# Strassen's seven products for the output GEMM of the second MLP too

## The chip, the core and the metric

The kernel runs on one core of a Trainium2 chip. Five engines work side by side: TensorE (PE) multiplies into PSUM banks, and its weight loads (PEld) overlap with it; VectorE (DVE), ScalarE (ACT) and GpSimd (POOL) compute on tiles; SyncE (SP) issues most DMAs. The metric is the device time of the whole program in microseconds; lower is better.

## The reference

Three stages run one after the other. Attention has 8 batches and 8 heads over 576 positions of 64 channels, with keys and values averaged in groups of 8. Its result is reshaped to 4608 rows of 512 and goes through two MLPs, all in float32:

```python
h = x @ w_in                                   # first MLP, 512 -> 2048 -> 512
g = np.where(h >= 1, h, np.where(h <= -1, 0.0, (h + 1) ** 2 / 4))
x = (g @ w_out).astype(np.float32)
gate = 1.0 / (1.0 + np.exp(-(x @ w_gate)))     # second MLP, 512 -> 1536 -> 512
val = x @ w_val
return (gate * val @ w_out).astype(np.float32)
```

## The kernel before

**Arithmetic.** Float32 values are split into a high and a low fp32r part: ScalarE writes the high part by a cast, VectorE the low part by a subtraction. `three` multiplies such pairs in three matmuls of 128x128 weights by 512 columns (high by high, high by low, low by high), so that any term costs three of them.

**Stages.** The 4608 rows are nine blocks of 512 (`TB`), kept transposed. Attention and the first MLP end at about 930 us of the trace. In the second MLP, block 0 is done plainly (`prepare`, `out_part`). Meanwhile `prepare` forms, for each of six groups `i` of two hidden tiles (`MP` = 6) and for gate and value (`n`), the seven weight combinations of Strassen's scheme in Winograd's form, and spills them to `seven` in HBM, 1792 KB for each `i` and `n`. Blocks 1 to 8 are then done in four pairs (`pr`).

**A pair.** Both input GEMMs use the seven products: for each `i` and `n` there are seven calls of the inner `product`, of six matmuls each. That is 6 x 2 x 7 x 6 = 504 matmuls a pair. Each product starts in one of four banks, `h` or `a`; VectorE adds (`add`) join the products outside PSUM, ScalarE copies one of them out (L917), and `finish` adds, takes the sigmoid (ScalarE, L903) or multiplies by it (VectorE, L910) into a `gs` tile. The output GEMM is plain: for each block and each of 12 hidden tiles, `out_part` splits `gs` (ScalarE L781, VectorE L782) and `three` adds into four `acc` banks, 2 x 12 x 4 x 3 = 288 matmuls a pair. Then `out_rows` copies the four banks to SBUF and stores rows of 512 floats.

**What sets the order.** Each call of `op` or `op2` records an operation with an engine, a cost, a due time (`key`), and the tiles that it reads and writes. `Plan.issue` then simulates the engines and writes every engine's instructions in the order in which its own times let them start, earliest due time first among those that could start together. On the chip each engine runs its list strictly in that order and waits on semaphores. The weights of one (`i`, `n`) come back in a single DMA (`load_seven`) to the three slots `wa`, `wa`, `wb`; SP's list holds these loads, the loads of `y` blocks and the stores.

Of the kernel before, what the change touches and what calls it, by code (L numbers as in the profile page):

```python
# [8 lines left out]
F32 = mybir.dt.float32  # L9
# [9 lines left out]
P = 128  # L19
# [45 lines left out]
class Plan:  # L65
# [7 lines left out]
    def op(self, eng, cost, key, fn, r=(), w=(), after=(), behind=(), nbytes=0, share=1.0, dmas=1):  # L73
# [24 lines left out]
        o.data, o.order = data, order - data  # L98
# [98 lines left out]
def pooled_attention_two_mlps(  # L197
# [46 lines left out]
    one, att, two = ExitStack(), ExitStack(), ExitStack()  # L244
# [424 lines left out]

    pools2 = {}  # L670

    def second_a():
        att.close()
        pools2["wa"] = two.enter_context(tc.tile_pool(name="wa", bufs=2))

    def second_b():
        one.close()
        pools2["right"] = two.enter_context(tc.tile_pool(name="two", bufs=1, side="right"))

    open_a = op("none", 0.0, 0.0, second_a, behind=att_ops)  # L680
    open_b = op("none", 0.0, 0.0, second_b, behind=one_ops)

    def late(tag, bufs, shape, dtype=F32, fifo=True):

        b = Buf(lambda: pools2["wa" if tag == "wa" else "right"], tag, bufs, shape, dtype, fifo)
        b.behind = [open_a if tag == "wa" else open_b]
        return b
# [5 lines left out]
    def buf_win(behind):  # L693
        b = Buf(win_p, "win", M1, [P, 2, TB], F32R)
        b.behind = behind
        return b
# [12 lines left out]
    PSTEP = 11 * 2.6  # L709
# [55 lines left out]
    def load_seven(n, i, key):  # L765
        sl, d = buf_seven(), seven[2 * i + n]
        op2(SP, 0.475, key, lambda: nc.sync.dma_start(
            out=sl.t.rearrange("p s k f -> p (s k f)").bitcast(F32), in_=d.t), r=[d], w=[sl], nbytes=P * 2 * NMAT * HK * 4)
        return sl
# [9 lines left out]
    def out_part(gs, m, key, accs, last, ahead=5):  # L779
        g = buf_g()  # L780
        op2(ACT, 0.62, key - ahead, lambda: nc.scalar.copy(out=g.t[:, 0], in_=gs.t), r=[gs], w=[g])  # L781
        op2(DVE, 0.69, key - ahead + 1, lambda: nc.vector.tensor_tensor(  # L782
            out=g.t[:, 1], in0=gs.t, in1=g.t[:, 0].bitcast(F32), op=ALU.subtract), r=[gs, g], w=[g])
# [6 lines left out]

    def buf_gs():
        return late("gs", 12, [P, TB], fifo=False)
# [9 lines left out]
    accs = [bank("acc") for _ in range(4)]  # L802
    for i in range(MP):
        slots = [prepare(n, i, due2(0, 2 * i) - 6 + 2.6 * n) for n in range(2)]
        T = due2(0, 2 * i)
        banks = {(n, f): bank("ha"[n], True) for n in range(2) for f in range(2)}
        for n in range(2):
            sl, a21 = slots[n]
            for f in range(2):
                last = []  # L810
                for c in range(KD):
# [5 lines left out]
                    last = [op(PE, 0.65, T + 5.2 * n + 2.6 * f + 0.1 * c, mm, r=[sl, a21, xs[c]], w=[banks[n, f]], behind=last)]  # L817
        for f in range(2):
            m = 2 * i + f
            t, gs = Buf(t_p, "t", 2, [P, TB]), buf_gs()  # L820
# [149 lines left out]
```

## Time and profile before

| what | value |
|---|---|
| median of 3 runs | 1752.68 us |
| the profiled execution | 1755.67 us |
| its span, first to last instruction | 1753.8 us |
| mean granted clock of TensorE | 0.995 |
| DMA, mean over the span | 134 GB/s |

The profiled execution took 3.0 us more than the median. A busy PE in the page is not PE at its peak, since the records of successive matmuls overlap; the spacing of their starts tells the pace. Times in the trace count from the first instruction.

### The profile page before, as it was taken

To read this page: it belongs to the slowest core of one execution; us is meant where nothing else is said; L and a number is where in the kernel's file an instruction comes from. 1 tells how busy PE (TensorE), PEld (TensorE's weight loads), DVE (VectorE), ACT (ScalarE), POOL (GpSimd) and SP (SyncE) were. 2 spreads that over 40 slices of the span, in tenths; PEclk is the share of its full clock that TensorE was granted. 3 is DMA by queue.
4 is the path that set the end of the run, shared out by engine and by line. 5 is a ranking of instruction groups with operands and counts; after the bars stand their busy time and mean duration, and the time that the engine had idled before them with its cause. 6 is when DMAs were issued, how large, how long until landed. Compare 5 with 4: busy or idle time off the path is not lost.

```text
span 1753.8 us, 24039 instructions
## 1 busy us (share of the span) xinstructions
PE 1723.8 (98%) x9016; PEld 1393.4 (79%) x9016; DVE 1051.5 (60%) x1874; ACT 805.7 (46%) x1786; POOL 52.7 (3%) x90
## 2 busy tenths in 40 slices
PE   7899999999999999999999999999999999999998
PEld 5676777778777778777887888888888888888887
DVE  5899867677776867574646645345444644464432
ACT  5876656566665656564755332123222312141212
POOL 0000001010010101010000000000000000000000
PEclk9999999999999999999999999999999999999999
DMA  7742525243443414031415875354344433443411
GB/s 205 229 119 69 149 57 163 62 134 97 116 116 92 134 45 134 16 128 40 174 39 202 318 291 204 126 192 145 126 146 166 149 119 146 166 167 126 150 43 49
DMA packets 148532, 234.37 MB, mean 134 GB/s; under 512 B 84160, under 2 KB 104640, under 8 KB 140736
## 3 DMA queue, kind: packets, MB, share of 16 engines
q1 hardware_dynamic: 138624, 182.50, 33.1%
q0 software_dynamic: 9792, 50.34, 7.9%
q8 instruction: 71, 1.16, 0.3%
q14 instruction: 45, 0.37, 0.1%
HBM read 173.02 MB, written 50.33 MB: 127 GB/s over the span
## 4 chain that ended last, share of the span: by engine, by line
PE 92%; DMA 3%; DVE 2%; ACT 1%; SPq 0%; issue 0%; DVEq 0%; ACTq 0%
PE acc L580 13%; PE h L580 13%; PE acc L582 13%; PE acc L581 13%; PE h L582 13%; PE h L581 12%; PE a L582 4%; PE a L581 4%; PE a L580 4%; PE a L484 2%; DMA raw<-in_moe_w_out_dram 1%; PE a L413 1%; DMA kv<-in_v_dram 1%; DMA x<-in_v_dram 1%; DMA xb<-y 0%
## 5 line engine op out<-in xcount | busy, mean ns | idle before, releaser
L580 PE MATMUL h<-x,win 128*128 128x512 f32 x576 | 231.2, 401 | 1.0 <-ACT win L505 1.0
L580 PE MATMUL acc<-g,wj 128*128 128x512 f32 x576 | 228.7, 397 | 1.2 <-ACT g L505 1.2
L582 PE MATMUL acc<-g,wj 128*128 128x512 f32 x576 | 225.4, 391 | 3.5 <-DVE wj L514 3.5
L582 PE MATMUL h<-x,win 128*128 128x512 f32 x576 | 225.7, 392 | 1.3 <-DVE win L514 1.3
L581 PE MATMUL acc<-g,wj 128*128 128x512 f32 x576 | 225.6, 392 | 1.0 <-DVE g L514 1.0
L581 PE MATMUL h<-x,win 128*128 128x512 f32 x576 | 225.5, 391 | 0.0
L781 ACT CAST g<-gs 128x512 fp32r<-128x512 f32 x108 | 66.8, 622 | 319.2 <-PE acc L582 200.4
L645 ACT ACTIVATE t<-h,half 128x512 f32<-128x512 f32 x144 | 99.2, 689 | 186.9 <-PE h L582 186.9
L582 PE MATMUL acc<-win,g 128*128 128x512 f32 x432 | 168.2, 389 | 2.1 <-DVE g L782 2.1
L580 PE MATMUL acc<-win,g 128*128 128x512 f32 x432 | 168.2, 389 | 0.0
L581 PE MATMUL acc<-win,g 128*128 128x512 f32 x432 | 168.1, 389 | 0.0
L782 DVE TENSOR_TENSOR g<-gs,g 128x512 fp32r<-128x512 f32 x108 | 74.1, 690 | 135.2 <-ACT g L781 135.0
L649 DVE SCALAR_TENSOR_TENSOR t<-t,h 128x512 f32<-128x512 f32 x144 | 97.3, 676 | 90.9 <-ACT t L647 90.8
L580 PEld LDWEIGHTS h<-x,win 128*128 128x128 f32 x576 | 108.7, 189 | 35.7 <-issue 9.7
L582 PEld LDWEIGHTS acc<-g,wj 128*128 128x128 f32 x576 | 108.4, 188 | 28.4 <-DVE wj L514 5.4
L580 PEld LDWEIGHTS acc<-g,wj 128*128 128x128 f32 x576 | 108.2, 188 | 27.8 <-ACT g L505 1.7
L582 PEld LDWEIGHTS h<-x,win 128*128 128x128 f32 x576 | 108.7, 189 | 25.9 <-DVE win L514 2.5
L581 PEld LDWEIGHTS acc<-g,wj 128*128 128x128 f32 x576 | 108.3, 188 | 23.2 <-DVE g L514 1.6
L581 PEld LDWEIGHTS h<-x,win 128*128 128x128 f32 x576 | 108.8, 189 | 21.1
L514 DVE TENSOR_TENSOR wj<-wout_f,wj 128x512 fp32r<-128x512 f32 x144 | 99.0, 688 | 33.3 <-ACT wj L505 33.0
L514 DVE TENSOR_TENSOR g<-t,g 128x512 fp32r<-128x512 f32 x144 | 98.8, 686 | 33.6 <-ACT g L505 33.1
L505 ACT CAST g<-t 128x512 fp32r<-128x512 f32 x144 | 89.1, 619 | 52.5 <-DVE t L649 50.1
(212 smaller groups left out, 3231.1 us busy)
## 6 DMA issues: line engine op xcount, KB each, us to landing
wa<-seven SPq DMA_DIRECT2D x32, 1792.0 KB
wb<-seven SPq DMA_DIRECT2D x16, 1792.0 KB
seven<-wa POOLq DMA_DIRECT2D x8, 1792.0 KB, 7.4
y<-raw SPq DMA_DIRECT2D x18, 512.0 KB
w<-f POOLq DMA_DIRECT2D x36, 256.0 KB, 2.5
out_dram<-raw SPq DMA_DIRECT2D x18, 512.0 KB
win<-in_moe_w_in_dram SPq DMA_DIRECT2D x16, 512.0 KB
raw<-in_moe_w_out_dram SPq DMA_DIRECT2D x16, 512.0 KB
```

Source lines behind the costliest of these rows:

```text
L413: nc.tensor.matmul(out=scs[h].t[r0 % P:r0 % P + D, r0 // P * C:r0 // P * C + C], lhsT=qT.t[D * h:D * h + D, r0:r0 + D], rhs=kts[b % 2, p]. ...
L484: nc.tensor.matmul(out=px.t[D * h:D * h + D, lo:hi], lhsT=vps[b % 2, p].t[:, h], rhs=rhs, start=True, stop=True)
L505: ACT: (0.52, lambda: nc.scalar.copy(out=dst.t[:, 0], in_=src())),
L514: op(engs, [0.6 if e == DVE else 1.23 for e in engs], key, [lambda e=e: by[e].tensor_tensor(out=dst.t[:, 1], in0=src(), in1=dst.t[:, 0].bi ...
L580: nc.tensor.matmul(out=o, lhsT=wh, rhs=xh, start=start, stop=False, skip_group_check=more)
L581: nc.tensor.matmul(out=o, lhsT=wh, rhs=xl, start=False, stop=False, skip_group_check=more)
L582: nc.tensor.matmul(out=o, lhsT=wl, rhs=xh, start=False, stop=stop, skip_group_check=more)
L645: op(ACT, 0.69, Tg, lambda t=t, hps=hps: nc.scalar.activation(out=t.t, in_=hps.t, func=AF.Relu, bias=half.t, scale=0.5), r=[hps, half], w=[t])
L649: op(DVE, 0.69, Tg + 2, lambda t=t, hps=hps: nc.vector.scalar_tensor_tensor(out=t.t, in0=t.t, scalar=1.0, in1=hps.t, op0=ALU.min, op1=ALU. ...
L781: op2(ACT, 0.62, key - ahead, lambda: nc.scalar.copy(out=g.t[:, 0], in_=gs.t), r=[gs], w=[g])
L782: op2(DVE, 0.69, key - ahead + 1, lambda: nc.vector.tensor_tensor(out=g.t[:, 1], in0=gs.t, in1=g.t[:, 0].bitcast(F32), op=ALU.subtract), r ...
```

## The change

The output GEMM of the four pairs goes by seven products too. A block of two hidden tiles and 512 outputs is a two by two of 128x256 blocks of the weight; the two blocks of the pair and the two hidden tiles make the other two by two. `out_pair` forms, in place in the tiles `hs` that hold the gated values, four combinations for each `i` (`sums`; VectorE or GpSimd, whichever the planner finds earlier), splits each operand afresh (L716, L717), and runs seven products of 6 x 6 matmuls, 252 a pair. Weights are now the stationary side, so results stand transposed and are turned on the way out: by VectorE's 32x32 block transposes with stores of 64 floats a row (`store`), or, for the last block half of all, by eight transposes on TensorE (`store_rows`).

`prepare_out` forms the seven combinations of the output weights during the first pair, from six reloads, and spills 42 tiles of 256 KB (`seven_o`). In the last pair the sixth and seventh products change places.

Where one product is to be added to another that is still needed alone, ScalarE copies the first from its bank into the next bank (`to_bank`) and TensorE adds the next product to it there. The gate and value products are rearranged in the same way. The weights of these come one product at a time (256 KB, 10 slots `ws`, rows of 1 KB), after the big slots `wa` and `wb` are closed (`second_c`). The combinations of the inputs (`minus`) may go to GpSimd. The planner's step for one `i` of a pair's input products is 27.3 us instead of 28.6 us (`PSTEP`).

```diff
-    PSTEP = 11 * 2.6
+    PSTEP = 10.5 * 2.6
+    def second_c():
+        zero.close()
+        zero_a.close()
+        pools2["ws"] = two.enter_context(tc.tile_pool(name="ws", bufs=10))
+        pools2["g2"] = two.enter_context(tc.tile_pool(name="g2", bufs=3))
+        pools2["wo"] = two.enter_context(tc.tile_pool(name="wo", bufs=5, side="right"))
...
+    def load_seven(n, i, mat, key):
+        w, d = late("ws", 10, [P, 2, HK], F32R), seven[2 * i + n]
+        op2(SP, 0.475, key, lambda: nc.sync.dma_start(
+            out=w.t.bitcast(F32), in_=d.t.rearrange("p (s k f) -> p s k f", s=2, k=NMAT)[:, :, mat]), r=[d], w=[w], nbytes=P * 2 * HK * 4)
...
+    def prepare_out(i, key):
+        a = Buf(raw_p, "raw", 2, [P, 4, HK], fifo=False)
+        sm = late("o", 2, [P, 4, HK])
...
+        comb(0, lambda: a.t[:, 1], lambda: a.t[:, 3], ALU.add)
+        comb(1, lambda: sm.t[:, 0], lambda: a.t[:, 0], ALU.subtract)
+        comb(2, lambda: a.t[:, 0], lambda: a.t[:, 1], ALU.subtract)
+        comb(3, lambda: a.t[:, 2], lambda: sm.t[:, 1], ALU.subtract)
+        for k in range(NMAT):
...
+            op2(PL, 1.0, key + 2 + k, lambda w=w, k=k: nc.gpsimd.dma_start(
+                out=seven_o[i][k].t, in_=w.t.rearrange("p s f -> p (s f)").bitcast(F32)), r=[w], w=[seven_o[i][k]], nbytes=P * 2 * HK * 4)
...
+    def out_pair(pr, hs, K0):
+        KP = PSTEP * MP / NMAT
...
+        def comb(key, h, n, x, y, alu, other=None):
+            op2((DVE, PL), (0.69, 1.3), key, [lambda e=e: by[e].tensor_tensor(out=h.t[:, n], in0=x(), in1=y(), op=alu) for e in (DVE, PL)],
+                r=[h] + ([other] if other else []), w=[h])
...
+        def product(n, mat, o, start, what):
+            chain = []
+            for i in range(MP):
+                key = K0 + KP * (n + i / MP)
...
+                split_to(key - 30, lambda src=src, b=b: src.t[:, b], lambda g=g: g.t[:, 0], lambda g=g: g.t[:, 1], 0.66, src, g)
...
+        def store(key, j, half, ct):
+            tr = Buf(raw_p, "raw", 2, [P, TB // 32, 2, 32])
+            for e in range(2):
+                op2(DVE, 0.63, key, lambda e=e: nc.vector.transpose(
+                    out=tr.t[:, :, e], in_=ct.t[:, e].rearrange("p (t i) -> p t i", i=32)), r=[ct], w=[tr])
+            for bl in range(4):
+                c0 = 2 * P * half + 64 * bl
+                op2(SP, 0.65, key + 20, lambda bl=bl, c0=c0: nc.sync.dma_start(
+                    out=out[j * TB:(j + 1) * TB, c0:c0 + 64].rearrange("(t j) i -> j t i", j=32),
...
+        product(0, 0, X, True, lambda k, h1, h2: (h1, 0))
+        s1 = o_buf()
+        to_sbuf(key(1) - 30, X, s1)
...
+        X2 = [bank("acc", True) for _ in range(2)]
+        to_bank(key(3) - 29, s1, X2)
...
+        product(4, 4, X2, False, lambda k, h1, h2: (h1, 0))
+        ct = c_buf()
+        add(key(5) - 30, ct, X2, s35)
...
+            Y2 = fourth()
+            ct = c_buf()
+            add(key(n4 + 1) - 30, ct, Y2, u3)
+            store_rows(key(n4 + 1) - 20, j1, 1, ct)
...
                 product(0, A, 0, B11, True)
-                op(ACT, 0.6, T + H * 1, lambda s1=s1, A=A: nc.scalar.copy(out=s1.t, in_=A.t), r=[A], w=[s1])
-                product(1, Bk, 4, T2, True)
-                add(T + H * 2, u2, Bk, s1)
-                product(2, Ck, 5, T3, True)
-                add(T + H * 3, u3, Ck, u2)
-                product(3, Dk, 3, T1, True)
-                finish(T + H * 4, (1, 1), Dk, u3)
-                product(4, A, 1, B21, False)
-                finish(T + H * 5, (0, 0), A, None)
-                product(5, Ck, 2, T4, False)
-                finish(T + H * 6, (1, 0), Ck, u2)
-                product(6, Dk, 6, B22, False)
-                finish(T + H * 7, (0, 1), Dk, u2)
...
+                to_bank(T + H * 1, A, Bk)
+                product(1, Dk, 3, T1, True)
+                op2(ACT, 0.6, T + H * 2 + 0.6, lambda u5=u5, Dk=Dk: nc.scalar.copy(out=u5.t, in_=Dk.t), r=[Dk], w=[u5])
+                product(2, Bk, 4, T2, False)
+                to_bank(T + H * 3, Bk, Ck)
+                op2(ACT, 0.6, T + H * 3 + 1, lambda u2=u2, Bk=Bk: nc.scalar.copy(out=u2.t, in_=Bk.t), r=[Bk], w=[u2])
+                product(3, A, 1, B21, False)
+                finish(T + H * 4, (0, 0), A, None)
+                product(4, Ck, 5, T3, False)
+                finish(T + H * 5, (1, 1), Ck, u5)
+                product(5, Dk, 6, B22, False)
+                finish(T + H * 6, (0, 1), Dk, u2)
+                product(6, Ck, 2, T4, False)
+                finish(T + H * 7, (1, 0), Ck, None)
```

What ScalarE's list holds in the third pair, while the products of that pair run, before (L903 sigmoids, L917 the copy of the first product to SBUF, L781 a high part for the output GEMM):

```order
L781 CAST g<-gs 128x512
L903 ACTIVATE t<-t 128x512
L903 ACTIVATE t<-h 128x512
L903 ACTIVATE f<-f 128x512
L781 CAST g<-gs 128x512
L903 ACTIVATE f<-f 128x512
L917 COPY f<-h 128x512
L781 CAST g<-gs 128x512 x2
L917 COPY f<-h 128x512
```

And in the changed kernel at the same place (L1113 `to_bank`, L1121 and L1124 copies to SBUF, L1102 sigmoids, L716 a high part for the output GEMM; `h` and `a` are PSUM banks):

```order
L1113 COPY h<-a 128x512
L1124 COPY u<-a 128x512
L1102 ACTIVATE t<-h 128x512
L1102 ACTIVATE t<-t 128x512
L1102 ACTIVATE f<-f 128x512
L1102 ACTIVATE f<-h 128x512
L1113 COPY a<-h 128x512
L716 CAST g_13215<-win 128x512
L1121 COPY u<-a 128x512
L1113 COPY h<-a 128x512
L1124 COPY u<-a 128x512
```

One copy a group of seven products became four, and two of them fill a bank that TensorE goes on with.

VectorE's list there before (L891 `add`, L910 the product with the sigmoid, L782 a low part):

```order
L891 TENSOR_TENSOR f<-a,u 128x512
L891 TENSOR_TENSOR u<-a,f 128x512
L891 TENSOR_TENSOR u<-h,u 128x512
L782 TENSOR_TENSOR g<-gs,g 128x512
L891 TENSOR_TENSOR gs<-a,u 128x512
L910 TENSOR_TENSOR gs<-gs,t 128x512
L910 TENSOR_TENSOR gs<-h,t 128x512
L891 TENSOR_TENSOR gs<-h,u 128x512
L910 TENSOR_TENSOR gs<-gs,f 128x512
```

And in the changed kernel (L1090 and L1107 `add`, L1109 the product with the sigmoid, L717 a low part, L883 a combination of `sums`):

```order
L1090 TENSOR_TENSOR t<-h,u 128x512
L1090 TENSOR_TENSOR f<-a,u 128x512
L717 TENSOR_TENSOR g<-win,g 128x512
L717 TENSOR_TENSOR g_14135<-win,g_14135 128x512
L883 TENSOR_TENSOR win<-win 128x512
L717 TENSOR_TENSOR g<-win,g 128x512
L883 TENSOR_TENSOR win<-win 128x512
L1109 TENSOR_TENSOR gs<-h,t 128x512
L717 TENSOR_TENSOR g_14206<-win,g_14206 128x512
L1107 TENSOR_TENSOR gs<-h,u 128x512
```

Three of five adds of a group are gone from VectorE; low parts are more, and combinations stand between.

The end of VectorE's list before (`raw` a staging tile of `out_rows`):

```order
L891 TENSOR_TENSOR gs<-h,u 128x512
L910 TENSOR_TENSOR gs<-gs,f 128x512
L782 TENSOR_TENSOR g<-gs,g 128x512 x3
L891 TENSOR_TENSOR gs<-a,u 128x512
L910 TENSOR_TENSOR gs<-gs,f 128x512
L598 COPY raw<-acc 128x512
L782 TENSOR_TENSOR g<-gs,g 128x512 x10
```

And in the changed kernel (L909 adds from banks `acc` to a staging tile, L916 block transposes, L938 a copy of turned results from bank `h`):

```order
L717 TENSOR_TENSOR g_16225<-win,g_16225 128x512
L909 TENSOR_TENSOR raw<-acc,o 128x512 x2
L916 STREAM_TRANSPOSE raw<-raw 128x16x32 x2
L717 TENSOR_TENSOR g<-win,g 128x512
L909 TENSOR_TENSOR raw<-acc,o 128x512 x2
L938 COPY raw<-h 128x512
```

At the end VectorE now adds twice and copies once behind the last low part, where before only ScalarE's copies followed.

## Rows read from the trace of the kernel before

**Rows 1.** The page: busy time by engine, granted clock, chain that ended last.

```profile
PE 1723.8 (98%) x9016; PEld 1393.4 (79%) x9016; DVE 1051.5 (60%) x1874; ACT 805.7 (46%) x1786; POOL 52.7 (3%) x90
...
PEclk9999999999999999999999999999999999999999
...
PE 92%; DMA 3%; DVE 2%; ACT 1%; SPq 0%; issue 0%; DVEq 0%; ACTq 0%
```

**Rows 2.** Windows, one pair long: PE, PEld, DVE, ACT, POOL busy, clock, DMA, GB/s.

```profile
1170.00:1349.50 179.50, 179.50 (x794) 148.68 (x793) 87.06 (x132) 48.01 (x81) 0.00 (x0) 1.00 0.42 150
1349.50:1529.00 179.50, 179.50 (x794) 148.68 (x793) 87.06 (x133) 48.00 (x81) 0.00 (x0) 1.00 0.41 149
```

**Rows 3.** Timeline of PE in the first pair: start us, us, instruction.

```profile
1099.68 0.39 PE L580 MATMUL a<-xb,wa 128*128 128x512 f32 x1
...
1112.83 0.39 PE L581 MATMUL acc<-win,g 128*128 128x512 f32 x1
```

**Rows 4.** Waits of PE from 900 us to 1750 us: total, times, longest.

```profile
PE acc L582 <- DVE g L782: 2.1, 1, 2.1
PE h L580 <- ACT t L821: 1.0, 1, 1.0
```

**Rows 5.** Timelines of PE, ACT and DVE: hand-overs from engine to engine.

```profile
1101.50 0.39 PE L582 MATMUL h<-x,wa 128*128 128x512 f32 x1
...
1101.98 0.59 ACT L917 COPY f<-h 128x512 f32<-128x512 f32 x1
...
1102.86 0.39 PE L582 MATMUL a<-x,wa 128*128 128x512 f32 x1
...
1103.36 0.69 DVE L891 TENSOR_TENSOR u<-a,f 128x512 f32<-128x512 f32 x1 [2.10 <-PE a L582]
...
940.57 0.60 ACT L821 ACTIVATE t<-h 128x512 f32<-128x512 f32 x1
...
941.22 0.50 PE L580 MATMUL h<-x,wb 128*128 128x512 f32 x1 [1.01 <-ACT t L821]
```

**Rows 6.** Timelines of PE and ACT, and the chain, at the end.

```profile
1748.86 0.39 PE L582 MATMUL acc<-win,g 128*128 128x512 f32 x1
...
1747.24 2.62 ACT L597 COPY raw<-acc 128x512 f32<-128x512 f32 x4 [5.50 <-PE acc L582]
...
1749.28 0.58 ACT raw L597
```

**Rows 7.** Groups by line from 850 us on: busy, mean ns, idle before.

```profile
L781 ACT CAST g<-gs 128x512 fp32r<-128x512 f32 x108 | 66.8, 622 | 319.2 <-PE acc L582 200.4 <-DVE gs L910 88.1 <-DVE gs L823 30.4
...
L917 ACT COPY f<-h 128x512 f32<-128x512 f32 x48 | 28.2, 587 | 66.2 <-PE h L582 65.0
...
L700 ACT CAST f<-f 128x256 fp32r<-128x256 f32 x10 | 4.0, 401 | 0.0
...
L782 DVE TENSOR_TENSOR g<-gs,g 128x512 fp32r<-128x512 f32 x108 | 74.1, 690 | 135.2 <-ACT g L781 135.0
...
L891 DVE TENSOR_TENSOR u<-h,u 128x512 f32<-128x512 f32 x48 | 33.2, 692 | 26.6 <-PE h L582 26.3
...
L751 DVE TENSOR_TENSOR raw<-f,wa 128x256 f32<-128x256 f32 x6 | 2.6, 425 | 7.5 <-DMA wa<-w 7.4
```

**Rows 8.** Timeline at the start: four transposes on PE, one select on POOL.

```profile
6.26 1.12 PE L384 MATMUL acc<-ident,q 128*128 128x128 f32 x4
...
1.02 0.29 POOL masks.py:199 TENSOR_SCALAR_AFFINE_SELECT ident<-ident 128x128 f32<-128x128 f32 x1
```

**Rows 9.** DMA: the page's queues and sizes, landing times, a window's share and GB/s.

```profile
DMA packets 148532, 234.37 MB, mean 134 GB/s; under 512 B 84160, under 2 KB 104640, under 8 KB 140736
...
q1 hardware_dynamic: 138624, 182.50, 33.1%
...
w<-f POOLq DMA_DIRECT2D x36, 256.0 KB, 2.5
...
5.00:30.00 25.00, 0.86 0.97 260
```

More of the change, by code (lines that the diff above doesn't have):

```diff
@@ L241, in pooled_attention_two_mlps @@
           "a": (ctx.enter_context(tc.tile_pool(name="ps_a", bufs=2, space=PSUM)), 2)}
-    one, att, two = ExitStack(), ExitStack(), ExitStack()
+    one, att, two, zero, zero_a = (ExitStack() for _ in range(5))
     edge = ctx.enter_context(tc.tile_pool(name="edge", bufs=1, side="right"))
@@ L801, in pooled_attention_two_mlps @@
         x_split(xs[c], due1(NB * M1 - 2))
-    accs = [bank("acc") for _ in range(4)]
+    accs, wb_slots = [bank("acc") for _ in range(4)], []
     for i in range(MP):
         slots = [prepare(n, i, due2(0, 2 * i) - 6 + 2.6 * n) for n in range(2)]
+        wb_slots += [x for x, _ in slots]
         T = due2(0, 2 * i)
@@ L825, in pooled_attention_two_mlps @@
-            out_part(gs, m, due2(0, m) + 2 * S2 + 5.2, accs, lasts)
+            op2(DVE, 0.69, T + 2.6 * f + 6, lambda t=t, f=f, gs=gs, pv=banks[1, f]: nc.vector.tensor_tensor(
+                out=gs.t[:, f], in0=pv.t, in1=t.t, op=ALU.mult), r=[t, banks[1, f]], w=[gs])
+            out_part(gs, f, m, due2(0, m) + 2 * S2 + 5.2, accs, lasts)
     out_rows(due2(0, M2 + 1) + 6, out[0:TB, :], accs)
+    open_c = op("none", 0.0, 0.0, second_c, behind=[u for x in wb_slots for u in x.users])
+    opens["wo"] = opens["ws"] = opens["g2"] = open_c
@@ L845, in minus @@
             u = late("u", 3, [P, TB])
[L846 to L847 removed]
+            op2((DVE, PL), (0.69, 1.3), key, [lambda e=e: by[e].tensor_tensor(
+                out=u.t, in0=x().bitcast(F32), in1=y().bitcast(F32), op=ALU.subtract) for e in (DVE, PL)], r=reads, w=[u])
             return u
@@ new lines, in to_bank @@
+                def to_bank(key, src, dst):
+                    op(ACT, 0.6, key, lambda: nc.scalar.copy(out=dst.t, in_=src.t), r=[src], w=[dst])
+                A, Dk, Bk, Ck = bank("h", True), bank("a", True), bank("a", True), bank("h", True)
+                u5, u2 = late("u", 3, [P, TB]), late("u", 3, [P, TB])
+                product(0, A, 0, B11, True)
+                to_bank(T + H * 1, A, Bk)
+                product(1, Dk, 3, T1, True)
+                op2(ACT, 0.6, T + H * 2 + 0.6, lambda u5=u5, Dk=Dk: nc.scalar.copy(out=u5.t, in_=Dk.t), r=[Dk], w=[u5])
```

194 lines of the change are left out of this document (147 added, 47 removed).

## The prediction

> **What bounds the kernel now.** I read the page first [rows 1]: PE is busy for 98% of the span, the granted clock is at full speed in every slice, and the chain that ended last is 92% PE. Busy time alone proves little, so the windows and the timeline come next. In two stretches one pair long [rows 2] PE has no gap at all, while VectorE is busy for 87.1 of 179.5 us and ScalarE for 48.0. The pace is in the starts [rows 3]: from 1099.68 to 1112.83 us lie 58 starts, so a matmul of 512 columns costs 13.15 / 58 = 0.2267 us, whatever it reads and whichever bank it fills. A pair before is 792 such matmuls, 792 x 0.2267 = 179.5 us, as long as the windows that I chose for it. The list of waits from 900 us on [rows 4] has two entries, 3.1 us in all, both in block 0. So the pairs are limited by the number of matmuls and by nothing else, and the question is whether the changed kernel can keep that pace.
>
> **Matmuls removed.** The output GEMM falls from 288 to 252 matmuls a pair, so 4 x 36 = 144 go: 144 x 0.2267 = **-32.6 us**. Nothing else covers them, since PE has no gaps there. The input products are as many as before.
>
> **The end, added.** Before, the last matmul starts at 1748.86 us, ScalarE copies the last bank (0.58 us from 1749.28 us), and the span ends at 1753.8 us, 4.9 us after that start [rows 6]. The other three copies overlapped with PE. Now the last bank goes through two VectorE adds (0.69 us each by L891 [rows 7]), eight transposes on PE, and a copy. The first add starts while PE is still on the second bank, so only about 1.2 us after the last start are the adds done. Four transposes take 1.12 us [rows 8], eight 2.2 us; then a copy of 0.69 us and hand-overs bring it to about 4.4 us after the last start, against 1.0 us before. The store afterwards is of the same kind. That is **+3.4 us**; between +2 if the copies and the first store overlap better, and +5 if the queue of small stores ahead delays the last.
>
> **Banks filled by ScalarE.** In the changed order, products 2 and 4 of a group add to a bank which ScalarE must first fill from the product two places ahead, and product 6 reuses the bank that a VectorE add has just read. Each has one product, 6 x 0.2267 = 1.36 us, of cover. What does such a hand-over take? From the end of the last matmul to ScalarE is 0.09 us (1101.50 + 0.39 to 1101.98), to VectorE 0.11 us (1102.86 + 0.39 to 1103.36), and back to PE 0.05 us (940.57 + 0.60 to 941.22) [rows 5]. Counted from the start of that matmul, PE may resume after 0.39 + 0.09 + 0.59 + 0.05 = 1.12 us behind ScalarE and 0.39 + 0.11 + 0.69 + 0.05 = 1.24 us behind VectorE. Without a wait it would resume after 0.23 + 1.36 = 1.59 us. So 0.47 us are spare on ScalarE and 0.35 us on VectorE, if the engine is free at that moment. A copy from bank to bank is not in the trace; the nearest is the bank-to-SBUF copy of 587 ns [rows 7], and it would have to be 0.47 us longer to matter.
>
> The engines are not always free. The order shows a high part on ScalarE ahead of a `to_bank`, and a low part on VectorE ahead of an add on which the next product waits. What is queued behind a late copy is the next group's whole row of copies, and PE waits for the first. A whole operation in the way (0.62 us, L781; 0.69 us [rows 7]) costs 0.15 us on ScalarE and 0.34 us on VectorE. With 48 groups, two such places on ScalarE and one on VectorE, the bounds are 0 and 96 x 0.15 + 48 x 0.34 = 31 us. By count, ScalarE has about 48 + 35 us of work in a pair of now 171 us: 36 more copies (21 us), 18 more high parts (11 us), and some 6 us of output copies, less the copies of `out_rows`. VectorE loses 36 adds (25 us) and gains 18 low parts, some 15 combinations, 6 adds and 7 transposes (32 us). On either, about a quarter to 40% of the time goes to work outside the groups, half of that with too short a rest to hurt. I take a tenth of the bound, **+3 us**, nearer zero: the planner puts other matmuls in when a product is not ready, and before it left no waits at all from 950 us on [rows 4].
>
> A place where a rule speaks against the change: 53 combinations go to GpSimd, whose largest elementwise row is a select of 128 columns in 0.29 us [rows 8]; four times the columns give an estimate of 1.15 us. The Trainium skill (SBUF — State Buffer, "Who interferes with whom") says that a VectorE instruction with two SBUF inputs and a GpSimd one that reads SBUF share a port that is locked for the whole instruction, so that the later one stands still. No run here has both at once. By it, 53 x 1.15 us would be added to VectorE in the worst case; as only a bank-reusing add delays PE, one such place in a group of 14.3 us, perhaps one hold in eight would reach PE for half a microsecond, 3 us in all. I leave that out of the sum.
>
> **First pair.** `prepare_out` adds six sets of 4 combinations and 7 splits, at 0.40 us on ScalarE and 0.42 us on VectorE for 128x256 [rows 7]: 17 us and 28 us in the first pair, beside 42 stores of 256 KB from GpSimd, 2.5 us each to landing [rows 9], through five buffers. A cast that waits for its buffer holds up ScalarE's list, the bank copies included. The nearest rows are the waits in block 0, where twelve larger sets are prepared: 3.1 us [rows 4]. Between 0 and 6; I take **+2 us**. The old two waits I keep: what precedes them in the program is little changed. If they go, it is -3.1 us.
>
> **Last pair.** The output products of the last pair have no input products beside them, and the swapped order puts two in a row on the same two banks: the second of them waits for VectorE's add from each. The first bank's add runs under the second's last three matmuls, so the wait is one add less that cover, 0.3 to 1.5 us; with the row of operands (a high part, a low part, sometimes a combination every 1.36 us, which VectorE can just follow) I take **+1 us**.
>
> **Transfers.** A pair moves 84 + 42 weight tiles of 262144 bytes, 2.6 MB of inputs and 2.1 MB of results: 37.7 MB in 171.4 us, 220 GB/s, against 150 GB/s [rows 2]. The page's queue q1 moved 182.5 MB in 33.1% of 16 engines' 1753.8 us [rows 9], which is 314 GB/s while busy, though more than half of all packets are under 512 B; the poorest busy window, at the start, ran at 260 GB/s. Ten slots reach 13.6 us of PE work ahead, and a tile lands in about 2.5 us. I take 0. Results of blocks leave in pieces of 256 B, and the Trainium skill (DMA: Bandwidth & Descriptors, "Specifications") wants at least 512 B for line rate, below which the engine reads, modifies and writes. If that doubles the cost of 2.1 MB a pair, the demand is that of 39.8 MB, 232 GB/s, still under both rates; the sum stays.
>
> **Sum.** -32.6 + 3.4 + 3 + 2 + 1 = -23.2 us. The profiled execution took 1755.67 us, so its like takes 1732.5; the median stood 3.0 us lower, so **1729 us**, 1.3% faster.
>
> **Rivals.**
> 1. *Nothing new waits, and the old waits go.* For it: the planner has hidden all such hand-overs in the pairs so far. Against: the cover shrank from two products to one. -32.6 + 2 - 3.1 = -33.7 us: 1719 us. This is the floor, and it is still short of 2%.
> 2. *The hand-overs eat the gain.* If every place meets a whole operation, +31 us in place of +3: 1757 us, no gain. For it: ScalarE's list is now in PE's loop twice a group, and it is nearly twice as full. Against: half its time is still free.
> 3. *Transfers set the pace (slower).* SP's list serves weights, output weights and stores in one row, in pieces of 1 KB and 256 B where rows of 14 KB came before. It decides from below 220 GB/s on. At 195 GB/s a pair takes 37.7 / 0.195 = 193 us instead of 171, 4 x 22 = 88 us more: 1817 us; slower than before by 2% from about 201 GB/s down. Against: 260 and 314 GB/s [rows 9].
> 4. *GpSimd's combinations hold up VectorE.* If VectorE stands still for the 1.15 us of each of the 53, a row of operands that VectorE can just follow slips in the last pair, and in the others a hold now and then reaches an add on which PE waits; at 0.1 to 0.2 us a hold that is 5 to 10 us, 1734 to 1739 us. For it: in the order, VectorE's subtractions of two SBUF tiles stand beside them. Against: no row of before has the two at once. It is the rule of the Trainium skill's page SBUF — State Buffer that is named above.
>
> **How the numbers follow.** The forecast 55%, rival 1 15%, rival 2 (from 1745 us up) 13%, rival 3 6%, rival 4 11%. The range runs from 1719 us, the floor, to 1751 us, which takes in four fifths of the bound on the hand-overs; beyond lie the rest of rival 2, rival 3 and what I overlooked. About 2% is what a measurement of this kernel can tell from no change: faster needs less than 1718.3 us, under the floor, 5%; slower needs more than 1787.7 us, rival 3 and a little of rival 2, 7%; within 2%, 88%.
>
> **What would show it.** In the changed profile: 144 fewer matmuls at the same 0.2267 us; PE waits in the pairs of under 10 us in all, for L1113 and for L1107 or L1090; the tail from the last 512-column matmul to the end 8 us; ScalarE about 80 us busy in a pair; DMA share about 0.6 in the pairs and no wait of PE on `ws` or `wo`. The prediction is wrong if PE waits for `ws` or `wo` loads, if a bank-to-bank copy takes over 1 us, or if the waits for ScalarE exceed 15 us.

## The result, and the profile after

The changed kernel takes **1766.39 us** (median of 8; before 1752.66 in the same comparison): ratio 1.007, 95% interval 1.0055 to 1.0086. That is 37 us above the forecast of 1729, above the range, and on the other side of no change. One of the eight runs of the kernel before took 2150.89 us and is not in the ratio. The profiled execution took 1764.11 us with a span of 1762.3 us.

The page of the changed kernel: busy time by engine, the granted clock, packets and queue q1, the landing time of one store.

```profile
PE 1704.5 (97%) x8880; PEld 1367.9 (78%) x8880; DVE 1121.1 (64%) x1963; ACT 950.9 (54%) x2064; POOL 165.2 (9%) x187
...
PEclk9999999999999999999999999999999999999999
...
DMA packets 290176, 292.70 MB, mean 166 GB/s; under 512 B 123776, under 2 KB 230784, under 8 KB 288512
...
q1 hardware_dynamic: 276896, 229.72, 45.5%
...
seven_o<-wo POOLq DMA_DIRECT2D x42, 256.0 KB, 5.3
```

Against [rows 1], TensorE has 136 fewer matmuls (144 removed, 8 transposes added) and 19 us less work, but the span grew by 8.5 us. So some 28 us of idle time is new, and TensorE's busy time fell by 13 us less than 32.6. The page cannot say where; windows can. Windows of 20 us, columns as in [rows 2]:

```profile
1200.00:1220.00 20.00, 20.00 (x90) 16.53 (x89) 7.70 (x12) 6.95 (x12) 0.00 (x0) 1.00 0.66 192
...
1320.00:1340.00 20.00, 15.52 (x66) 11.91 (x65) 17.40 (x25) 12.07 (x21) 8.78 (x6) 1.00 0.84 268
1340.00:1360.00 20.00, 13.90 (x50) 9.51 (x49) 20.00 (x19) 7.22 (x13) 13.84 (x9) 0.91 0.55 154
...
1520.00:1540.00 20.00, 15.04 (x51) 10.03 (x51) 20.00 (x22) 9.60 (x18) 13.79 (x9) 0.91 0.63 183
```

In the middle of a pair the pace of 90 matmuls in 20 us holds. At the passage from one pair to the next it drops to 66, 50 and 51, and GpSimd is busy. In the last two of these windows VectorE has no gap at all, yet completes only 19 and 22 instructions in 20 us. Over the twenty windows of 40 us from 940 to 1740 us, twelve hold 177 to 179 matmuls; what the others lack against 178 adds up to 202, times 0.2267 = 45.8 us, against 18 matmuls, 4.1 us, before. Of the 202, 159 lie at the three passages, 17 in the last pair (1700 to 1740 us) and 22 in the first window, where the 18 of before lie too. The row of the kernel before at the second passage:

```profile
1340.00:1380.00 40.00, 40.00 (x178) 33.15 (x177) 28.34 (x45) 17.93 (x32) 0.00 (x0) 1.00 0.53 184
```

And the row of the changed kernel there:

```profile
1340.00:1380.00 40.00, 33.27 (x135) 25.57 (x135) 28.38 (x31) 14.61 (x26) 13.84 (x9) 0.96 0.56 161
```

VectorE is as long busy (28.34 and 28.38 us), with 31 instructions in place of 45: 0.92 us each against 0.63. The waits of TensorE, 850 to 1763 us, in total, times, longest, name VectorE first, where [rows 4] had two entries of 3.1 us:

```profile
PE acc L581 <- DVE g L717: 11.5, 6, 2.7
PE h L581 <- DVE x L712: 4.1, 3, 1.8
PE h L580 <- DVE t L1090: 3.2, 2, 2.5
PE h L580 <- ACT h L1113: 2.9, 2, 2.5
```

Why is VectorE slow there? The timeline of VectorE in the changed kernel at that passage:

```profile
1338.42 0.64 DVE L717 TENSOR_TENSOR x<-u,x 128x512 fp32r<-128x512 f32 x1
...
1339.59 1.77 DVE L717 TENSOR_TENSOR win<-u,win 128x512 fp32r<-128x512 f32 x1
1341.29 1.77 DVE L712 TENSOR_TENSOR xb<-xb 128x512 fp32r<-128x512 f32 x1
...
1345.99 3.45 DVE L717 TENSOR_TENSOR win<-u,win 128x512 fp32r<-128x512 f32 x2
```

GpSimd's timeline beside it:

```profile
1339.14 1.67 POOL L1040 TENSOR_TENSOR u<-xb,u 128x512 f32<-128x512 f32 x1 [0.71 <-DVE x L717]
1340.78 1.73 POOL L883 TENSOR_TENSOR win<-win 128x512 f32<-128x512 f32 x1
```

The subtraction that takes 0.64 us at 1338.42 takes 1.77 us at 1339.59. GpSimd's instruction of 1339.14 ends at 1340.81, VectorE's at 1341.36; the next pair ends at 1342.51 and 1343.06. Each time VectorE is done 0.55 us after GpSimd: it stood still until GpSimd was through, and then did its work. From 1333 to 1352 us there are seven such instructions, some 1.08 us too long each, 7.6 us of 19. An add on VectorE that has one of its inputs in a bank is not held in the middle of GpSimd's work (VectorE's row, then GpSimd's):

```profile
1541.36 0.68 DVE L1090 TENSOR_TENSOR f<-a,u 128x512 f32<-128x512 f32 x1
...
1539.18 3.41 POOL L883 TENSOR_TENSOR gs<-gs 128x512 f32<-128x512 f32 x2
```

GpSimd is held as well. With nothing on VectorE beside it a combination takes 1.30 us, as the planner assumed:

```profile
1119.39 1.30 POOL L883 TENSOR_TENSOR gs<-gs 128x512 f32<-128x512 f32 x1
```

The one of 1339.14 started 0.15 us after a subtraction on VectorE (L712), which ended at 1339.66; it ended at 1340.81, 1.15 us later. So the 1.65 to 1.73 us seen at the passages are 1.3 us of work and some 0.4 us of standing still. The groups of VectorE in the changed kernel from 850 us on (columns as in [rows 7]):

```profile
L717 DVE TENSOR_TENSOR g<-win,g 128x512 fp32r<-128x512 f32 x126 | 95.2, 765 | 93.2 <-ACT g L716 93.2
...
L717 DVE TENSOR_TENSOR x<-u,x 128x512 fp32r<-128x512 f32 x16 | 18.1, 1129 | 0.0
L717 DVE TENSOR_TENSOR win<-u,win 128x512 fp32r<-128x512 f32 x16 | 17.8, 1117 | 0.0
...
L712 DVE TENSOR_TENSOR xb<-xb 128x512 fp32r<-128x512 f32 x8 | 9.8, 1226 | 0.0
```

And GpSimd's, the largest group and the one with the longest mean (one of its five took 4.62 us):

```profile
L883 POOL TENSOR_TENSOR win<-win 128x512 f32<-128x512 f32 x29 | 48.1, 1676 | 166.7 <-DVE g L717 166.7
...
L1040 POOL TENSOR_TENSOR u<-xb 128x512 f32<-128x512 f32 x5 | 10.9, 2174 | 24.2 <-DVE win L717 17.0 <-ACT t L831 6.0 <-issue 1.3
```

A wait can cost more than itself. One window of 4 us of the changed kernel (the clock is the third number from the end):

```profile
1348.00:1352.00 4.00, 2.48 (x6) 1.89 (x7) 4.00 (x4) 3.01 (x6) 2.77 (x3) 0.62 0.30 81
```

TensorE's timeline there:

```profile
1349.52 0.80 PE L580 MATMUL h<-x,ws 128*128 128x512 f32 x1 [2.50 <-ACT h L1113]
1350.12 0.63 PE L581 MATMUL h<-x,ws 128*128 128x512 f32 x1
...
1352.54 0.39 PE L581 MATMUL a<-xb,ws 128*128 128x512 f32 x1
```

After idling for 2.5 us, at the end of a stretch with waits of 2.22, 0.64 and 1.70 us, TensorE starts seven matmuls in 3.02 us where 7 x 0.2267 = 1.59 would do: the granted clock is 0.62 in that window (0.50 from 1350 to 1352 us), with most starts 0.42 us apart, the 1.2 GHz level. So this wait cost 1.4 us beyond its 2.5. Not every such wait does. This one, ten microseconds later, left the clock at 1.00, and the next starts are 0.33 and 0.23 us apart:

```profile
1360.64 0.50 PE L580 MATMUL h<-win,ws 128*128 128x512 f32 x1 [2.48 <-DVE t L1090]
```

From 940 us on, four windows of 20 us show a clock of 0.91 (from 940, 1160, 1340 and 1520 us); up to 1740 us the kernel before has none. At some 1.4 us each that is an estimated 5 to 6 us. In such stretches TensorE is busy for longer with the same matmuls, which is one reason why its busy time fell by less than 32.6 us.

The end, which was costed by hand, in the timeline of the changed kernel:

```profile
1755.34 0.39 PE L582 MATMUL acc<-g,ws 128*128 128x512 f32 x1
...
1756.51 0.99 PE L933 MATMUL h<-id,raw 128*128 128x128 f32 x7 [0.29 <-DVE raw L909]
1757.53 0.59 ACT L937 COPY raw<-h 128x512 f32<-128x512 f32 x1 [8.82 <-PE h L933]
```

From the last start to the span's end are 7.0 us, against 4.9 before [rows 6]: +2.0. The sum over the span is then 1753.8 - 32.6 + 2.0 = 1723.2 us, and 39 us are lost against it, most of them at passages.

### The profile page after: what moved, and what is told of

Its sections match the earlier page's. It is cut to its first block, busy times and chain, and to the rows that moved or that the text cites. A ratio compares the mean times of both kernels' runs of the same rounds, so it can differ in the third digit from the quotient of the medians.

```text
span 1762.3 us, 25582 instructions
## 1 busy us (share of the span) xinstructions
PE 1704.5 (97%) x8880; PEld 1367.9 (78%) x8880; DVE 1121.1 (64%) x1963; ACT 950.9 (54%) x2064; POOL 165.2 (9%) x187
## 5 line engine op out<-in xcount | busy, mean ns | idle before, releaser
L717 DVE TENSOR_TENSOR g<-win,g 128x512 fp32r<-128x512 f32 x126 | 95.2, 765 | 93.2 <-ACT g L716 93.2
L716 ACT CAST g<-win 128x512 fp32r<-128x512 f32 x126 | 78.1, 622 | 82.1 <-PE acc L582 66.5
L581 PE MATMUL acc<-g,wo 128*128 128x512 f32 x288 | 112.7, 391 | 8.9 <-DVE g L717 8.9
L581 PE MATMUL h<-x,ws 128*128 128x512 f32 x288 | 113.8, 395 | 4.1 <-DVE x L712 4.1
L580 PE MATMUL h<-x,ws 128*128 128x512 f32 x288 | 113.5, 394 | 3.6 <-ACT h L1113 2.9
```

What stands on the lines that cost most here:

```text
L580: nc.tensor.matmul(out=o, lhsT=wh, rhs=xh, start=start, stop=False, skip_group_check=more)
L581: nc.tensor.matmul(out=o, lhsT=wh, rhs=xl, start=False, stop=False, skip_group_check=more)
L716: op2(ACT, cost, key, lambda: nc.scalar.copy(out=out_hi(), in_=val()), r=[src, b], w=[b])
L717: op2(DVE, cost, key + 0.5, lambda: nc.vector.tensor_tensor(out=out_lo(), in0=val(), in1=out_hi().bitcast(F32), op=ALU.subtract), r=[src, ...
```

## The experiments

Two questions were put. First: is it GpSimd's use of SBUF that stretches VectorE (theory A), GpSimd's own slowness and the order made for it (B), or VectorE's plain load at the passages, whoever else works (C)? Then: what is left without GpSimd? Ratios are to the kernel before, beside which each ran, with 95% intervals. "Kernel 2" is the kernel of run 2, "kernel 8" that of run 8.

**1. The same instructions on VectorE.** Every combination that the planner gave to GpSimd stays in its place and is issued on VectorE.

```diff
-  ... for e in (DVE, PL)]        (comb and minus)
+  ... for e in (DVE, DVE)]
```

> The 53 combinations that the changed kernel gives to GpSimd stand at the same places of the order, but on VectorE. Theory A (a VectorE instruction with two SBUF inputs stands still while GpSimd reads SBUF): the low parts fall from 765 ns back to 690 ns, PE waits after 930 us fall from 31 us to under 10, time 1728 to 1738 us. Theory B (GpSimd is simply slower, 1.65 us, than the 1.3 us planned, and its results come late): also 1728 to 1738 us. Theory C (VectorE has too much to do where one pair passes into the next, whoever else works): 53 x 0.69 = 37 us more on VectorE, PE waits stay above 25 us, time 1755 us or more.

1749.81 us, 0.9971 (0.9958 to 0.9984). VectorE has 53 instructions more, and the kernel is 1% faster than the changed one, 17 us. VectorE's subtractions are back at their length (`g<-win,g` at 686 ns):

```profile
L717 DVE TENSOR_TENSOR x<-u,x 128x512 fp32r<-128x512 f32 x16 | 10.8, 676 | 0.0
```

The direction is that of A and B, but the time lies between their range (1728 to 1738 us) and that of C, and TensorE's waits fall from 31 to 20 us, not under 10. So something is left that A does not explain.

**2. Planned without GpSimd.**

```diff
-  op2((DVE, PL), (0.69, 1.3), key, ...
+  op2((DVE,), (0.69,), key, ...
```

> The planner may use VectorE alone for the combinations of the inputs and of the gated values, and plans the order for that. A and B: 1726 to 1736 us, since the order now knows the work; at most 3 us better than the same order on VectorE. C: 1755 us or more.

1744.58 us, 0.9945 (0.993 to 0.996): 1.25% under the changed kernel, 22 us. This too is above the range that was expected.

**3. GpSimd writes and doesn't read.** A fill with zeros takes the place of each combination on GpSimd.

```diff
-  by[e].tensor_tensor(out=h.t[:, n], in0=x(), in1=y(), op=alu)   (on PL)
+  nc.gpsimd.memset(h.t[:, n], 0.0)
```

> GpSimd writes zeros into the same tiles at the same places and reads nothing, so the 53 combinations are left out of the result. A: only GpSimd's reads hold VectorE, so its low parts are back at 690 ns and the time is 1726 to 1736 us. If any work of GpSimd on SBUF holds VectorE, the low parts stay above 720 ns and the time above 1740 us. C: the time is near 1750 us, as the rest of VectorE's work is unchanged.

1736.72 us, 0.9902 (0.9886 to 0.9919). The upper end of the range is missed by 0.7 us. GpSimd keeps its 53 places, and VectorE is not held. GpSimd's group in this run:

```profile
L883 POOL MEMSET win<- 128x512 f32 x29 | 14.7, 523 | 178.0 <-DVE g L717 178.0
```

And one of VectorE's:

```profile
L717 DVE TENSOR_TENSOR x<-u,x 128x512 fp32r<-128x512 f32 x16 | 10.9, 680 | 0.0
```

A fill is also shorter (0.52 us against 1.68). But length alone would leave short holds, and there are none. A subtraction right beside a fill, in this run's timelines of VectorE and GpSimd:

```profile
1325.95 0.68 DVE L717 TENSOR_TENSOR x<-u,x 128x512 fp32r<-128x512 f32 x1
...
1325.96 0.53 POOL L883 MEMSET win<- 128x512 f32 x1
```

Beside GpSimd's reading, in the changed kernel, a VectorE subtraction that starts second ends 0.55 us after it. Run 3 is also 0.7% (12 us) faster than run 1, where the same places hold 53 instructions of VectorE. So VectorE's own time for them is not free, and theory C is right in part.

**4. The planner told the time that GpSimd took beside VectorE.**

```diff
-  op2((DVE, PL), (0.69, 1.3), key, ...
+  op2((DVE, PL), (0.69, 1.68), key, ...
```

> The planner is told 1.68 us for a combination on GpSimd instead of 1.3 us; 48 instead of 53 go there. A: VectorE is still held by nearly as many, 1755 to 1770 us. B: GpSimd's results come when they are planned, 1728 to 1740 us.

1769.86 us, 1.0087 (1.0072 to 1.0102). 48 combinations still go to GpSimd, and nothing is gained. Theory B falls: it is not an order made with a wrong duration, and 1.3 us was GpSimd's time when nothing held it. Nor did VectorE wait for GpSimd's results: before `x<-u,x` it had no idle time (0.0 above).

**5. The hold alone, in the kernel before.** Its 32 subtractions `minus` may go to GpSimd; 15 do.

```diff
-  op2(DVE, 0.69, key, lambda: nc.vector.tensor_tensor(
+  op2((DVE, PL), (0.69, 1.3), key, [lambda e=e: by[e].tensor_tensor(
```

> The kernel before, with one part of the change alone: the planner may give the combinations of the inputs to GpSimd, and gives it 15 of 32. If GpSimd's reads hold VectorE, the split subtractions of the inputs stretch from 0.69 us to 1.1 us and more here too; what that costs PE depends on what covers it: 12 output matmuls for one split, so 0 to 8 us, 1752 to 1761 us. If the hold needed Strassen's output products, VectorE's means stay at 0.69 us and the time at 1753 us.

1762.85 us, 1.0049 (1.0033 to 1.0064): +8.6 us from 15 instructions and the order planned with them, 2 us above the expected range, in a kernel that had hardly any waits there. The most stretched group of VectorE in this run:

```profile
L701 DVE TENSOR_TENSOR x<-x 128x512 fp32r<-128x512 f32 x16 | 17.4, 1094 | 0.6 <-POOL u L846 0.6
```

And of GpSimd:

```profile
L846 POOL TENSOR_TENSOR u<-xb 128x512 f32<-128x512 f32 x4 | 10.2, 2548 | 8.5 <-DVE win L706 8.5
```

GpSimd is held too: 2548 ns in the mean where 1.30 us is its time alone. Theory A stands: the cost goes with GpSimd's combinations into a kernel that has nothing else of the change.

**6. No sums.** Kernel 2 without the 96 combinations of `sums()`.

```diff
-  for i in range(MP):
-      f(key(at + i / MP), *hs[i])
+  return
```

> The changed kernel with VectorE alone for the combinations, and the 96 combinations of the gated values left out of the computation: the output products multiply the uncombined values. If what is left of the loss (1744.6 us with VectorE alone, against 1723 us if PE never waited) is VectorE's load where one pair passes into the next, 96 x 0.6 = 58 us less on VectorE bring it to 1728 to 1736 us. If the order of the lists or the bank copies are the cause, it stays at 1740 us or more.

1743.01 us, 0.9932 (0.9912 to 0.9951), which kernel 2 can't be told from. So the load of the sums, 24 VectorE instructions a pair, is not what is left in kernel 2.

**7. The new order of a group in the kernel before.** The seven products with `to_bank`, and nothing of the output GEMM.

```diff
-  op(ACT, 0.6, T + H * 1, ... s1 <- A)   product(1, Bk, 4, T2, True)   add(T + H * 2, u2, Bk, s1) ...
+  to_bank(T + H * 1, A, Bk)   product(1, Dk, 3, T1, True) ...
```

> The kernel before with the groups of seven input products rearranged as in the change, banks filled by ScalarE and all, and nothing else (one gated tile a pair stands in another pool for want of room). If a bank filled by ScalarE costs PE a wait by itself, up to 31 us: 1760 us or more. If the hand-over fits in the one product of cover, as the changed kernel's rows in mid-pair suggest: 1751 to 1756 us.

1757.17 us, 1.0012 (0.9999 to 1.0025): at most some 4 us. The waits of TensorE from 930 us on:

```profile
PE acc L582 <- DVE g L782: 2.0, 1, 2.0
PE acc L580 <- ACT raw L597: 1.5, 3, 0.7
```

No product waits for a bank that ScalarE fills. In the changed kernel the copy from bank to bank (L1113) takes 571 ns, and between 1180 and 1300 us TensorE has no gap. By themselves the hand-overs cost nothing that can be told from zero.

**8. The old order of a group in kernel 2.** The output GEMM by seven products alone.

```diff
-  to_bank(T + H * 1, A, Bk)   product(1, Dk, 3, T1, True) ...
+  op(ACT, 0.6, T + H * 1, ... s1 <- A)   product(1, Bk, 4, T2, True)   add(T + H * 2, u2, Bk, s1) ...
```

> The changed kernel with VectorE alone for the combinations, and the groups of input products in the order of before: no bank filled by ScalarE there, 144 adds more on VectorE. If ScalarE's bank copies, which stand in its list behind casts that wait for VectorE, are what PE waits for at the passage of the pairs, 1730 to 1740 us; if VectorE's load there decides, more adds make it worse: 1746 to 1760 us.

**1739.48 us, 0.991 (0.9886 to 0.9933)**: faster than both kernels, and the fastest of those that leave nothing out. The interval overlaps that of kernel 2; the medians differ by 5 us, though VectorE has 144 adds more. The waits of kernel 2 for ScalarE's copies (a and h by L1113, 3.2 us) are gone. The likely reading, which the overlap keeps from being firm, is that at a passage the copies stand in ScalarE's list behind casts that wait for VectorE.

The remaining loss is again at passages. The chain of this run from 1318 to 1345 us (start, us, what):

```profile
1323.69 4.42 DMA out_dram<-raw
...
1328.87 0.67 DVE raw L916
1329.54 0.57 DVE x L717
1330.11 1.80 DVE u L1040 x3
1331.92 0.61 DVE g L717
```

A store frees the tile that VectorE's transpose waited for; then inputs of the next pair stand ahead of the operand `g` on which TensorE waits. More than the two slots of `raw` were not tried.

**9. Larger pieces in the stores.** Kernel 8 with a block half stored by one transfer in pieces of 1 KB in place of four in 256 B (values land in other places).

```diff
-  for bl in range(4): ... out[...].rearrange("(t j) i -> j t i", j=32) ...
+  out[...].rearrange("(c p) d -> p c d", p=P) ...
```

> As the run with the output products alone (1739.5 us), but the turned results leave in pieces of 1 KB and one DMA instead of pieces of 256 B and four; the values land in other places of their block. Theory D (what is left is lost because transfers pile up where one pair passes into the next, small stores among them, so that the next inputs come late): 1728 to 1735 us, and the loads of x land sooner. If the small stores take nothing from the loads that matter: 1737 to 1742 us.

1736.47 us, 0.9909 (0.9882 to 0.9936): not to be told from kernel 8.

**10 and 11. The planner told the transfers' rate, then also the matmuls' time.**

```diff
-  o.bytes / o.dmas / 360e3
+  o.bytes / o.dmas / (270e3 if self.late else 360e3)      (10 and 11)
-  PSTEP = 10.5 * 2.6          op2(PE, 1.3, ...)
+  PSTEP = 10.5 * 2.72         op2(PE, 1.36, ...)           (11)
```

> As the run with the output products alone, but the planner counts 270 GB/s for transfers in the pairs instead of 360 GB/s, as the windows show there; the work is the same. If the order, made with transfers that are too fast, is what makes PE wait at the passage of the pairs: 1728 to 1736 us. If the work itself is too much there whatever the order: 1737 to 1745 us.

> In addition the planner counts 1.36 us for a product of six matmuls, as measured, instead of 1.3 us. Theory of the order: 1726 to 1735 us, no worse than with the slower transfers alone; theory of the load: 1737 to 1745 us.

1750.53 us, 0.9987 (0.9974 to 1.0001), and 1748.37 us, 0.9963 (0.9949 to 0.9977): both slower than kernel 8 and above what either theory expected. An order made with slower transfers is not a better one here; why it is worse was not followed up.

**12. More slots for output weights.** Kernel 8 with 7 of `wo` and 8 of `ws` in place of 5 and 10.

```diff
-  wo: bufs=5    ws: bufs=10
+  wo: bufs=7    ws: bufs=8
```

> As the run with the output products alone, with 7 instead of 5 slots for the output weights and 8 instead of 10 for the input weights. PE's waits for wo (3.7 us) go if they come from SP's list standing still for a free slot; then 1735 to 1738 us. If the transfers themselves are slow there, they stay, 1739 us.

1743.32 us, 0.9941 (0.9922 to 0.996). The range of 1735 to 1738 us is missed: the waits for `wo` go, others come (`ws` 2.5 us, `g` 6.9), and nothing is gained.

Two theories are left for the passages: the next pair's inputs are late (D), or the splits of the output operands are enough to be late by themselves (E).

**13. Inputs prepared once.** Kernel 8, with pair 1's split inputs used for all pairs.

```diff
+  if pr:
+      x7 = x7_0
-  for kt in range(2): x_raw(B11[kt], ...) ... x_split(b22, ...)
+  if pr == 0:
+      for kt in range(2): x_raw(B11[kt], ...) ... x_split(b22, ...)
```

> The kernel of e8_out_only (1739.5 us), with the preparation of the inputs of the later pairs left out: pair 1's split tiles x serve all four pairs (output values are then those of pair 1's inputs; 22 VectorE operations, 14 casts and 16 loads a pair fall away for three pairs). Theory D, that what still waits at a passage is the next pair's inputs queued on VectorE, ScalarE and the loads beside the output products: nearly all of the some 9 us of waits at the three passages go, and with the stretches of lower clock behind them, 1722 to 1730 us. Theory E, that the splits of the output operands are enough by themselves to be late: 1736 to 1741 us, and the waits remain.

**14. Output operands split once.** Kernel 8, one split tile a pair for all 42 steps.

```diff
-  split_to(key - 30, ... src, g)
+  if not held:
+      split_to(key - 30, ... src, g)
+      held.append(g)
```

> The kernel of e8_out_only, with the splits of the output operands left out: each pair's 42 output steps all read the first one's split tile (41 casts and 41 subtractions a pair fall away; output values are not the reference's). Theory E: 1722 to 1730 us. Theory D: the inputs' preparation still has its own chain of load, subtraction, cast and subtraction, but a freer VectorE and ScalarE; 1730 to 1738 us, with the waits for x left. If neither this nor the run with inputs prepared once gets below 1732 us, the weights' loads (wo) at the passages set what is left.

13: **1725.40 us**, 0.9836 (0.9815 to 0.9857). 14: **1727.44 us**, 0.9853 (0.9833 to 0.9873). Each of the two by itself brings the kernel to the floor of 1723.2 us of span, to within 2 us (spans of 1722.5 and 1725.4 us). The window at the second passage in kernel 8 (columns as in [rows 2]):

```profile
1330.00:1350.00 20.00, 16.73 (x63) 12.49 (x62) 18.62 (x32) 10.69 (x20) 0.00 (x0) 0.91 0.64 186
```

In run 13:

```profile
1330.00:1350.00 20.00, 20.00 (x90) 16.57 (x89) 17.67 (x29) 4.85 (x9) 0.00 (x0) 1.00 0.81 225
```

In run 14, with the window ahead of it:

```profile
1310.00:1330.00 20.00, 19.34 (x86) 15.68 (x85) 16.86 (x27) 5.02 (x9) 0.00 (x0) 1.00 0.92 295
1330.00:1350.00 20.00, 20.00 (x90) 16.57 (x89) 12.31 (x20) 8.16 (x14) 0.00 (x0) 1.00 0.80 239
```

So neither theory D nor E was right by itself: each expected that the other's load would leave waits, and hardly any are left. The engines that split can carry the inputs or the operands at pace, but not both at once. Which of them binds is not shown: both runs take casts off ScalarE as well as subtractions off VectorE, and of the runs that took work off VectorE alone, 3 gained 12 us against 1, and 6 nothing against 2. Transfers are not what is short: run 14 still loads every input and moves 295 GB/s at the passage with TensorE at 19.34 of 20 us. In run 13, though, ten loads a pair fall away with the arithmetic (the expectation's 16 was a miscount), so the part of x that matters (the loads' landing or VectorE's work on them) isn't parted.

**15 and 16. The same load at other times.** Kernel 8 with the inputs due 10 us earlier, or the output products 13.7 us later.

```diff
-  Tx = T0p - 4
+  Tx = T0p - 14                                        (15)
-  out_pair(pr, hs, T0p + PSTEP * (MP + 0.3))
+  out_pair(pr, hs, T0p + PSTEP * (MP + 0.8))           (16)
```

> The kernel of e8_out_only, with the planner's due times of the next pair's inputs 10 us earlier (Tx = T0p - 14 for - 4), nothing else. Theory D, if the order gives the inputs too little time: 1730 to 1737 us. If it is the buffers of x (16 slots, 10 for a pair) that hold the inputs back, due times change nothing: 1738 to 1742 us.

> The kernel of e8_out_only, with the output products of a pair due half an input step (13.7 us) later (K0 = T0p + PSTEP * (MP + 0.8) for + 0.3), so that they lie beside more of the next pair's input products and less beside its inputs' preparation. Theory D and E both: the load at the passage is spread, 1730 to 1738 us; against it, the last pair's output products have nothing beside them, which does not change. If the order is already bound by something else: 1738 to 1745 us.

1744.36 us, 0.9946 (0.9925 to 0.9966), and 1742.03 us, 0.9935 (0.9915 to 0.9956). Neither shift helps; in 15 the waits for `g` shrink from 4.7 + 0.7 to 2.3 us and those for x grow from 0.9 to 9.9. Whether the number of buffers of x and g binds both together was not tried.

## Why the prediction was wrong

**The step that failed** stands under "Banks filled by ScalarE", where 53 combinations on GpSimd were weighed and left out of the sum: "perhaps one hold in eight would reach PE for half a microsecond, 3 us in all". Its length was nearly right: 1.15 us assumed for GpSimd, 1.30 us measured alone and 1.08 us for a hold. In six groups of VectorE (`g<-win,g`, `g<-gs,g`, `x<-u,x`, `win<-u,win`, `x<-x`, `xb<-xb`) the changed kernel has at least 35 us more than the run without GpSimd, about 33 holds of 53. What was wrong is the share that reaches TensorE. The text held that only a bank-reusing add delays PE, as if the combinations lay evenly over a pair. But the longest of TensorE's waits are for split operands: 11.5 us for `g` (L717) and 6.4 us for x (L712, L717), against 3.2 us for an add (L1090). And the combinations lie mostly at the passages, where VectorE is busy for 20.00 of 20 us, so that most of a hold there makes TensorE late, and some of the waits bring 1.4 us at the lower clock on top. The cost is 22 us (1.0070 less 0.9945), 0.4 us a combination. Rival 4, with 11%, named the mechanism; its price of 0.1 to 0.2 us a hold was too low too, and its 1739 us is 27 us short.

The rule that was named there, of the Trainium skill's page SBUF — State Buffer ("Who interferes with whom"), is borne out: a subtraction of 0.68 us took 1.77 us, until 0.55 us after GpSimd's end, and fills that only write held nothing. The page says the same of GpSimd instructions that only write.

**A step that was missing**: the sum prices no collision of output operands with the next pair's inputs. By counts VectorE looked half idle. But an output operand is split for 6 matmuls now where it served 12 before, and 22 VectorE operations and 14 casts of inputs fall into the same 20 to 40 us. Runs 8 and 13 price it at 0.74%, 13 us. By which engine or buffer it comes about stays open.

**Banks filled by ScalarE** (+3, bounds 0 to 31): some 2 us by themselves (run 7, interval 0 to 4), perhaps 5 at the passages (run 8 against 2, overlapping intervals). The term was sized about right, and rival 2 is wrong: one product of cover was enough mid-pair.

**Matmuls removed**: right; 144 fewer, and the pace of 90 in 20 us holds mid-pair. Runs 13 and 14 show that the floor was real: 1752.7 - 32.6 + 2.0 = 1722.1 us against 0.9836 x 1752.7 = 1723.9 us.

**The end**: right in kind, +2.0 against +3.4; the adds were done 1.1 us after the last start, as forecast; the eight transposes took 1.6 us where 2.2 were assumed, and two engines share the last copies.

**First pair**: +2 was enough. In the changed kernel three of the four windows of 40 us from 980 to 1140 us hold 178 matmuls and one 177, although DMA is busy for 0.96 to 0.99 of the time from 1020 us on and a store lands in 5.3 us.

**Last pair**: the window from 1700 to 1740 us lacks 17 matmuls, 3.9 us, against +1. From 1660 to 1750 us TensorE waits 2.7 us for `g` (L717) and 0.7 us for a cast (L716). In runs 1, 2 and 3 the 0.7 us stay and the 2.7 us are gone, so without GpSimd's holds +1 was about right.

**Transfers**: right that they don't set the pace (rival 3 is wrong): TensorE waited once for `wo`, 0.7 us, and never for `ws`, and from 1180 to 1300 us, with 192 to 207 GB/s at a share of 0.67 to 0.74, TensorE has no gap. The 512 bytes that the Trainium skill (DMA: Bandwidth & Descriptors, "Specifications") asks for would have brought little: run 9 is not to be told from 8.

Of the signs given, the matmul count held, the tail was 7.0 us for 8, the copy from bank to bank took 0.57 us and the waits for ScalarE came to 7 us, under their limits of 1 and 15; the one wait for `wo` was to have been none. TensorE's listed waits were some 31 us where under 10 was expected, two fifths of them for VectorE's split of `g` (L717), which was not among the lines named.

The account: 22 us from GpSimd's combinations, some 5 from the new order at the passages, 13 from inputs and output operands together, 40 in all, for the 39 that the changed kernel lies above its floor. These are the steps of one row of runs (the changed kernel, 2, 8, 13) that ends at the floor, so that they add up proves nothing more, and the middle one rests on overlapping intervals. The 22 us are a net price: the work that GpSimd gives back costs VectorE time too (run 3 against 1).

## What to carry to other kernels

Load an engine by window, not by its mean: an engine with half its time free in a pair had none at the passage, and there most of an added microsecond goes through. Moving elementwise work from VectorE to GpSimd can take almost nothing off VectorE when both read SBUF at once: here 53 instructions of 0.69 us, 37 us, were moved, and at least 35 us of holds came back. The faster kernel kept all of it on VectorE. Halving the matmuls that one operand serves adds splitting beside them (42 splits a pair for 24), so ask at the busiest window whether the engines that split can follow.

## What was not expected of the hardware

- The hold goes both ways. GpSimd's `tensor_tensor` of 128x512 took 1.30 us alone, 1.65 to 1.73 us behind a VectorE subtraction, and 2.17 to 2.55 us in the mean of the groups that collided most; VectorE's, held by it, 1.77 us for 0.68.
- A fill by GpSimd (0.52 us) left VectorE's subtractions at 0.68 us, and GpSimd's reading left VectorE's adds from a bank at 0.68 us.
- One wait of 2.5 us, after others, was followed by seven starts in 3.02 us with TensorE at the 1.2 GHz level, 1.4 us more than the wait itself; another of 2.48 us was followed by full pace.
- A copy by ScalarE from one bank to another takes 571 ns, no more than from a bank to SBUF (586 ns, L958).
